# Joining attention bursts on TensorE and weaving strips of several products into them, with every engine's order written anew

## The chip, the cores and the metric

The kernel runs on one core of a Trainium2 chip. The metric is the time of one execution in microseconds (us), the median of several runs. A profile of one execution tells which engine did what and when.

## The reference

Four layers work on x, 2048 tokens of 448 numbers: sliding attention, a gated product, attention, a gated product. Each is added to its input after a layer norm without weights.

```python
def _A_ref(x, wqkv, wo):                 # H = 16 heads of Dh = 28; W, dil = 8, 2
    q, k, v = ...                        # x @ wqkv, split by head
    idx = pos[:, None] - (jnp.arange(W) * dil)[None, :]
    kg, vg = k[..., idx_c, :], v[..., idx_c, :]        # 8 keys and values for each token
    logits = jnp.einsum("bhsd,bhswd->bhsw", q, kg) * Dh ** -0.5     # masked where idx < 0
    o = jnp.einsum("bhsw,bhswd->bhsd", softmax(logits), vg)
    return o.transpose(...).reshape(B, S, D) @ wo
def _B_ref(x, w_gate, w_up, w_down):     # F = 1792
    return ((x @ w_gate) * (x @ w_up)) @ w_down
x = x + _A_ref(_layernorm(x), A_wqkv, A_wo)
x = x + _B_ref(_layernorm(x), B_w_gate, B_w_up, B_w_down)
# and both once more, with the same weights
```

Data are bf16.

## The kernel before

Tokens of even and odd position are kept apart, so that a key two positions back is the neighbour, and attention looks at a window of eight neighbours. Attention works on query blocks of 120 tokens (the first has 128), two blocks to a group, nine groups (0 to 8) in each of the two attention layers (0 and 2). The weight products work on chunks of 256 or 512 tokens. `SEQ` gives the chunks' order, in which the layers overlap: attention of chunk 1 stands ahead of the gated product of chunk 0, and so on.

**What each engine does.** TensorE computes the products for queries and keys (`WQK`), values (`WV`), attention's output (`wo_g`), gate and up (`WGU`) and down (`WD`). In all of these it is used as two tiles of 64 rows by 128 columns, and two matmuls, a pair, run at once (mode `R64`; line 351, function `pair`). For a group of attention it computes scores (line 826, `ps<-Qz,qk`, in `attn_front`) and then, of their exponentials, the attention values, AV for short (line 860, `ps<-E_sb,v_sb`, in `attn_back`). AV matmuls are 64 rows by 32 columns, eight tiles side by side; a group has 64 of them (group 0 has 32). Scores are in one of two forms, set by `WIDE_S`: a group named there has 32 matmuls in 64x64 tiles (group 0: 16), any other has 64 in 64x32 tiles (group 0: 32), each over fewer columns. Between scores and AV stand two exponentials on ScalarE (line 835) and two masks by VectorE (line 842). After the AV, copies (line 871), a sum (line 875), a shuffle of the denominators (line 885), a logarithm and an exponential (lines 886 and 887) and a product (line 898) give `oT`, which the output product reads. VectorE also does the layer norms (lines 571 to 592) and the sums into x (line 915); a gate result is copied out by ScalarE (line 951) and multiplied with the up result by VectorE (line 954). Copies of queries, keys (line 701) and values (line 793) out of PSUM go to ScalarE or VectorE, as the order says.

**Transposes.** A normed block of x is transposed for the products, in the head of the kernel by TensorE (line 606) and later by a DMA that SyncE issues (line 595). The last four heads' values reach their blocks through DRAM (lines 712 to 721), again by a transposing DMA.

**Bursts and strips.** A run of small attention matmuls between two products is a burst. Ahead of it and behind it TensorE changes tile size. In some bursts, strips of a product are woven in: a pair of the product is cut into eight 64x32 matmuls (line 354, `strip` in `pair`), which have the tile size of the attention matmuls, so the small ones and the strips follow each other without a change of size. The product that lends them is called the host; `alt` holds the strips of its first six pairs at most (`MAXALT`), and what is not in strips follows in pairs.

**What sets the order.** The order of every engine's operations is written out in the table `ORDER`, by operation numbers, and the PSUM banks of each TensorE operation in the table `BANKS`; `Sched.schedule` only reads them, and `emit` adds the waits that the dependences ask for. A word such as `545*1.2.4.5/434` in TensorE's order means: operation 545 (an AV) with host 434; after its first 8, 16, 32 and 40 matmuls comes one row of eight strips of 434 each. In this form a burst has one attention operation, or several before the cut (`762+776*...`), and one host.

Of the kernel before, what the change touches and what calls it, by code (L numbers as in the profile page):

```python
# [29 lines left out]
WIDE_S = ((0, 0), (0, 1), (0, 2), (0, 3), (0, 4), (0, 5))  # L30
MAXALT = 6
S_ORDER = (0, 4, 2, 6, 1, 5, 3, 7)
# [63 lines left out]
def grp_nc(g):  # L96
# [21 lines left out]
    ),  # L118
    "act": (
# [12 lines left out]
    ),  # L132
# [67 lines left out]
class Sched:  # L200
# [22 lines left out]
    def schedule(self):  # L223
# [9 lines left out]
        for e in self.ENGS:  # L233
            self.order[e] = []
            for w in ORDER[e].split():
# [4 lines left out]
                if k:  # L240
                    short, cut, host = seq, [8 * int(c) for c in k.split(".")], self.ops[int(host)]
                    got.append(host)
                    k = len(cut)
# [853 lines left out]
```

## Time and profile before

| | |
|---|---|
| three runs | 382.94, 383.2 and 385.03 us; median 383.2 |
| profiled execution, span from its first to its last instruction | 380.8 us |
| median less the span | 2.4 us |
| TensorE matmuls | 375.8 us busy (99%), 6322 |
| VectorE | 287.0 us busy (75%), 644 instructions |
| ScalarE | 203.6 us busy (53%), 389 instructions |
| granted TensorE clock, mean | 1.000 |

The profile has no time of its own execution besides the span, so the span stands beside the median of the runs.

Times are from the span's start. In a row of the timeline stand start, time, engine, line, instruction, output and inputs, the tile (rows*columns) and what streams through it, and how many instructions are merged in the row. The time of such a row ends with the last result of its last matmul, some 0.2 to 0.4 us after the next row may have begun, since matmuls are pipelined; so prices are taken from start to start. In the stretches' rows stand the stretch, its length, and for PE (matmuls), PEld (weight loads), DVE (VectorE), ACT (ScalarE) and POOL (GpSimd) the busy us with the count of instructions.

### The profile page before, as it was taken

What the parts mean: (1) busy time and instruction counts of PE and PEld (TensorE: products, weight loads), DVE (VectorE), ACT (ScalarE), POOL (GpSimd) and SP (SyncE); (2) the same over time, 40 slices, a digit from 0 to 9 for tenths busy, and PEclk for the clock granted to TensorE, in tenths of its full rate; (3) what the DMA queues carried; (4) which work ended last, traced back from release to release, by engine and by line L of the source; (5) the groups of instructions that cost most, each with busy time, mean ns of one, the idle gap of its engine ahead of it and who ended that gap; (6) DMA issues with size and microseconds to landing.
All of it is one profiled execution on the core that took longest, in us unless ns stands there. A gap on an engine that the chain in (4) does not pass through costs nothing.

```text
span 380.8 us, 14251 instructions
## 1 busy us (share of the span) xinstructions
PE 375.8 (99%) x6322; PEld 210.2 (55%) x6322; DVE 287.0 (75%) x644; ACT 203.6 (53%) x389; POOL 5.1 (1%) x25
## 2 busy tenths in 40 slices
PE   8999999999999999999999999999999999999997
PEld 4645587545445445444756765545555444446664
DVE  8988999999976786787677985637998598455323
ACT  5997987746426652564465525547744635133320
POOL 5000000000000000000000000000000000000000
DMA  8656533600611034031101125320125004140002
GB/s 263 163 148 177 106 94 95 80 19 3 99 29 33 2 65 58 16 67 26 32 14 34 20 43 101 39 45 4 28 34 74 3 2 78 23 120 26 3 2 98
DMA packets 54881, 22.50 MB, mean 59 GB/s; under 512 B 45012, under 2 KB 54820, under 8 KB 54820
## 3 DMA queue, kind: packets, MB, share of 16 engines
q1 hardware_dynamic: 54676, 21.53, 27.6%
q8 instruction: 50, 0.82, 0.9%
q14 instruction: 11, 0.09, 0.1%
q10 hardware_dynamic: 144, 0.06, 0.1%
HBM read 8.54 MB, written 2.71 MB: 30 GB/s over the span
## 4 chain that ended last, share of the span: by engine, by line
PE 94%; DVE 2%; ACT 1%; issue 1%; DMA 1%; SPq 0%; DVEq 0%
PE ps L351 85%; PE ps L354 3%; PE ps L860 2%; PE ps L826 2%; PE ps L966 1%; ACT E_sb L835 1%; DMA x_sb<-in_A_x_dram 1%; DVE xn_sb L592 1%; DVE st L571 0%; PE ps L606 0%; DVE Qz L812 0%; DVE R_sb L885 0%; DVE E_sb L842 0%; SPq L443 0%; DVE qk L701 0%
## 5 line engine op out<-in xcount | busy, mean ns | idle before, releaser
L351 PE MATMUL ps<-xnTb,WGU 64*128 64x512 bf16 (+1 forms) x1894 | 172.4, 332 | 0.0
L351 PEld LDWEIGHTS ps<-xnTb,WGU 64*128 64x128 bf16 x1894 | 92.0, 94 | 69.8 <-issue 1.4
L951 ACT ACTIVATE g_sb<-ps 128x512 bf16<-128x512 f32 (+1 forms) x140 | 70.1, 510 | 85.0 <-PE ps L351 65.5
L954 DVE TENSOR_TENSOR hT<-g_sb,ps 128x512 bf16<-128x512 bf16 (+1 forms) x140 | 78.2, 575 | 46.9 <-ACT g_sb L951 44.4
L351 PE MATMUL ps<-WD,hT 64*128 64x448 bf16 x812 | 82.8, 350 | 0.0
L351 PEld LDWEIGHTS ps<-WD,hT 64*128 64x128 bf16 x812 | 38.9, 94 | 34.7 <-DVE hT L954 0.3
L351 PE MATMUL ps<-xnTa,WQK 64*128 64x512 bf16 (+1 forms) x494 | 53.0, 353 | 0.5 <-DVE WQK L518 0.3
L915 DVE TENSOR_TENSOR x_sb<-x_sb,ps 128x448 bf16<-128x448 bf16 x62 | 37.2, 614 | 14.7 <-PE ps L351 14.4
L835 ACT ACTIVATE E_sb<-ps,shift_sb 128x1024 bf16<-128x1024 f32 (+1 forms) x36 | 37.0, 1068 | 12.6 <-PE ps L826 12.4
L571 DVE BATCH_NORM_STATS2 st<-x_sb 128x6 f32<-128x448 bf16 x64 | 38.6, 616 | 1.3 <-DMA x_sb<-in_A_x_dram 0.8
L592 DVE TENSOR_SCALAR xn_sb<-x_sb,mv,rstd 128x512 bf16<-128x512 bf16 (+1 forms) x64 | 35.2, 566 | 5.5 <-ACT rstd L576 5.5
L701 ACT ACTIVATE qk<-ps 128x1024 bf16<-128x1024 f32 (+1 forms) x29 | 27.1, 947 | 15.6 <-PE ps L351 15.6
L351 PEld LDWEIGHTS ps<-xnTa,WQK 64*128 64x128 bf16 x494 | 23.0, 94 | 21.6 <-DVE WQK L518 0.5
L351 PE MATMUL ps<-wo_g,oT 64*128 64x448 bf16 x250 | 28.6, 350 | 0.0
L842 DVE TENSOR_TENSOR E_sb<-E_sb,MK 128x1024 bf16<-128x1024 bf16 (+1 forms) x36 | 23.4, 658 | 5.3 <-ACT E_sb L835 5.2
L886 ACT ACTIVATE R_sb<-R_sb 128x480 f32<-128x480 f32 (+1 forms) x34 | 20.2, 601 | 9.6 <-DVE R_sb L885 9.6
L898 DVE TENSOR_TENSOR oT<-O_sb,R_sb 128x480 bf16<-128x480 f32 (+3 forms) x36 | 22.1, 624 | 4.3 <-ACT R_sb L887 4.2
L351 PE MATMUL ps<-WV,xnTa 64*128 64x336 bf16 (+3 forms) x252 | 24.2, 305 | 0.1
L885 DVE STREAM_SHUFFLE R_sb<-O_sb 128x480 f32<-128x480 f32 (+1 forms) x34 | 23.1, 692 | 0.0
L574 ACT ACTIVATE lnv<-mv,eps_sb 128x2 f32<-128x2 f32 (+1 forms) x33 | 9.3, 291 | 22.2 <-DVE mv L573 22.2
L887 ACT ACTIVATE R_sb<-R_sb 128x480 f32<-128x480 f32 (+1 forms) x34 | 20.2, 601 | 0.5
L871 ACT ACTIVATE O_sb<-ps 128x512 f32<-128x512 f32 (+3 forms) x18 | 9.8, 557 | 14.9 <-PE ps L860 14.9
(60 smaller groups left out, 214.8 us busy)
## 6 DMA issues: line engine op xcount, KB each, us to landing
out_dram<-x_sb SPq DMA_DIRECT2D x15, 112.0 KB, 1.8
x_sb<-in_A_x_dram SPq DMA_DIRECT2D x3, 448.0 KB, 5.8
hT<-in_A_wqkv_dram SPq DMA_DIRECT2D x4, 224.0 KB, 4.4
WGU<-in_B_w_gate_dram SPq DMA_DIRECT2D x4, 224.0 KB, 3.9
WGU<-in_B_w_up_dram SPq DMA_DIRECT2D x4, 224.0 KB, 3.8
WD<-in_B_w_down_dram SPq DMA_DIRECT2D x2, 448.0 KB, 4.2
WGU<-in_B_w_gate_dram SPq DMA_DIRECT2D x2, 336.0 KB, 4.8
WGU<-in_B_w_up_dram SPq DMA_DIRECT2D x2, 336.0 KB, 4.4
```

The source lines that it names most:

```text
L351: return lambda E: E.matmul(out(), lhs(), rhs(), start=start, stop=stop)
L571: sc.add("dve", one(lambda E, B=B: E.bn_stats(st6[:, B, :], x_sb[:, B, :]), ("bn", li, B)), 525.0, deps=[("x", li - 1, B)] + ([("xn", li - ...
L592: sc.add("dve", one(lambda E, B=B, dst=dst, src=src: E.tensor_scalar(dst, src, mv[:, B, 0:1], rstd[:, B:B + 1], ALU.subtract, ALU.mult), ( ...
L701: return E.activation(dst, src, ACT.Copy) if hasattr(E, "activation") else E.tensor_copy(dst, src)
L835: return E.activation(E_sb[:, slot, 2 * hp:2 * hp + 2, 0:w], ps[:, b0:b0 + 2, 0:w], ACT.Exp, bias=shift_sb[:, 0:1], scale=SCALE)
L842: return E.tensor_tensor(e, e, MK[:, kind, 0:nc].unsqueeze(1).unsqueeze(1).to_broadcast([128, 2, w // nc, nc]), ALU.min)
L885: sc.add("dve", one(lambda E: E.stream_shuffle(R_sb[:, rs, 0:w], O_sb[:, os_, 0:w], [DH] * 32), ("Rs", li, qb)), dve_est(w) + 20.0, deps=[ ...
L886: sc.add("act", one(lambda E: E.activation(R_sb[:, rs, 0:w], R_sb[:, rs, 0:w], ACT.Ln), ("Rl", li, qb)), act_est(w, False), deps=[("Rs", l ...
L898: return E.tensor_tensor(oT[:, :, a % HALF:a % HALF + z - a], O[:, :, a - tok:z - tok], R_sb[:, rs, 0:w].rearrange("p (h n) -> p h n", h=4 ...
L915: sc.add("dve", one(lambda E: E.tensor_tensor(x_sb[:, B, :], x_sb[:, B, :], ps[:, bk[w], 0:D], ALU.add), ("x", li, B)), dve_est(D), deps=[ ...
L951: sc.add("act", one(lambda E, gs=gs, bk=bk: E.activation(g_sb[:, gs, 0:nt], ps[:, bk[0], 0:nt], ACT.Copy), ("G", li, j, fc)), act_est(nt), ...
L954: sc.add("dve", one(lambda E, gs=gs, bk=bk, fc=fc: E.tensor_tensor(hT[:, fc, hs, 0:nt], g_sb[:, gs, 0:nt], ps[:, bk[1], 0:nt], ALU.mult), ...
```

## The change

Four things are changed.

1. `WIDE_S` holds group 0 of layer 0 alone. Groups 1 to 5 of layer 0 compute their scores with 64 matmuls in 64x32 tiles instead of 32 in 64x64 tiles.
2. `Sched.schedule` reads a wider form of a burst: several attention operations may be joined (`618+596`) and cut anywhere, and the strips may come from several hosts, each with the number of its pairs that are cut (`/729:2+484:6`).
3. The orders of all engines, SyncE's among them, are new, and with them the choice of ScalarE or VectorE for some copies and sums out of PSUM.
4. The banks are new.

The operations themselves, their sizes and their number are the same, but for the scores of point 1 and the pairs that are cut. In the built program TensorE has 6854 matmuls instead of 6322, 936 of them strips instead of 440. There are 31 bursts instead of 33, and the number of bursts without strips (the half groups included) falls from 15 to 6. The small product forms that are cut are now those of queries and keys, values, attention output, gate/up with 256 and 512 columns, and down.

```diff
-WIDE_S = ((0, 0), (0, 1), (0, 2), (0, 3), (0, 4), (0, 5))
+WIDE_S = ((0, 0),)
...
 ORDER = {
     "pe": (
...
-        "... 518 327 389 398 512 321 513 324 507 333 508 336 337 540*3.5/338 339 523 580 410 581 411 440 ... 545*1.2.4.5/434 ..."
-        "... 591*1.3.5/458 473 585 ... 596*1.2.4.5/654 669 681 666 482 613*2.4.5/483 660 ... 618*3.5/732 ..."
+        "... 518*4/281:1 327 333 388 512 389 398*1.3.4.6/507:2+513:2 508 336 337 580 540*1.2.3.4.5.6.7/338:1+339:6 410 581 523*2.4.6/411:3 ..."
+        "... 545*1.2.3.4.5.6.7/437:5+536:2 ... 591*1.3.4.6/477:3+558:1 ... 613*1.2.3.4.5.6.7/660:6+483:1 666 730 728 731 618+596*1.3.5.7.8.10.12.14/729:2+484:6 ..."
...
     "act": (
...
     "dve": (
...
     "sp": (
-        "... 511 90 427 429 510 433 516 431 576 577 578 515 583 579 574 ..."
+        "... 510 511 516 515 88 577 579 575 573 574 90 578 576 584 583 429 433 427 431 589 588 647 ..."
...
 BANKS = (
...
@@ schedule
                 w, _, tail = w.partition("*")
-                k, _, host = tail.partition("/")
+                k, _, tail = tail.partition("/")
                 got = [self.ops[int(i)] for i in w.split("+")]
                 seq = [(o, n) for o in got for n in range(len(o.ins))]
                 if k:
-                    short, cut, host = seq, [8 * int(c) for c in k.split(".")], self.ops[int(host)]
-                    got.append(host)
-                    k = len(cut)
-                    cut += [len(short)]
+                    short, cut = seq, [8 * int(c) for c in k.split(".")] + [len(seq)]
+                    hosts = [(self.ops[int(i)], int(n)) for i, n in (h.split(":") for h in tail.split("+"))]
+                    strips = [(o, i) for o, n in hosts for i in range(n)]
+                    assert len(strips) == len(cut) - 1
+                    got += [o for o, _ in hosts]
                     seq, a = [], 0
                     for i, z in enumerate(cut):
                         seq += short[a:z]
                         a = z
-                        if i < k:
-                            seq += [(host, host.alt[i][q]) for q in (S_ORDER if short[z - 1][0].acquire.n == 4 else range(8))]
-                    seq += [(host, n) for n in range(2 * k, len(host.ins))]
+                        if i < len(strips):
+                            o, j = strips[i]
+                            seq += [(o, o.alt[j][q]) for q in (S_ORDER if short[z - 1][0].acquire.n == 4 else range(8))]
+                    seq += [(o, n) for o, m in hosts for n in range(2 * m, len(o.ins))]
```

More of the change, by code (lines that the diff above doesn't have):

```diff
@@ L104 @@
     "pe": (
[13 rows of a table removed]
[15 rows of a table added]
     ),
     "act": (
[12 rows of a table removed]
[12 rows of a table added]
     ),
     "dve": (
[18 rows of a table removed]
[18 rows of a table added]
     ),
     "pool": (
-        "18 19 38 20 21 22 23 24 25 26 27 28 29 30 31 32 33 34 35 36 37"
+        "18 22 19 21 20 23 24 38 25 26 27 28 29 30 31 32 33 34 35 36 37"
     ),
     "sp": (
[5 rows of a table removed]
[5 rows of a table added]
     ),
```

128 rows, old and new, of tables (BANKS, ORDER) are left out of this document.

## The prediction

> **What bounds the kernel now.** I read the page first: busy shares, slices, chain of waits. Then the busy time by stretches, then the timeline of TensorE around single bursts, since the change is made of bursts.
>
> ```profile
> span 380.8 us, 14251 instructions
> ...
> PE 375.8 (99%) x6322; PEld 210.2 (55%) x6322; DVE 287.0 (75%) x644; ACT 203.6 (53%) x389; POOL 5.1 (1%) x25
> ...
> DVE  8988999999976786787677985637998598455323
> ...
> PE 94%; DVE 2%; ACT 1%; issue 1%; DMA 1%; SPq 0%; DVEq 0%
> ```
>
> TensorE is busy 99% of the span and 94% of the chain that ended last is TensorE's. So a microsecond less in TensorE's own stream is a microsecond less of span, as long as its inputs come in time. The row of 40 slices says where that may fail: VectorE is full for the first ten slices (95 us) and has room after that. By stretches (columns: stretch and length, then busy us and count of PE, PEld, DVE, ACT, POOL):
>
> ```profile
> 10.00:40.00 30.00, 29.53 (x544) 16.05 (x542) 27.08 (x80) 26.76 (x49) 0.00 (x0) 1.00 0.63 156
> 40.00:80.00 40.00, 39.30 (x882) 26.50 (x880) 39.18 (x92) 31.95 (x60) 0.00 (x0) 1.00 0.45 86
> 80.00:100.00 20.00, 20.00 (x354) 9.50 (x352) 18.27 (x40) 11.78 (x24) 0.00 (x0) 1.00 0.15 30
> ```
>
> From 40 to 80 us VectorE is busy 39.18 of 40. TensorE stands still for 0.47 us from 10 to 40 and 0.70 us from 40 to 80, then no more. So there are two bounds: both engines up to about 95 us, TensorE alone behind it.
>
> **What a burst costs.** A product runs in 64x128 tiles, two matmuls at a time (a pair). A burst is a run of small attention matmuls in 64x32 or 64x64 tiles. These rows (start, time, instruction) price bursts without strips:
>
> ```profile
> 37.41 0.64 PE L826 MATMUL ps<-Qz,qk 64*64 64x128 bf16 x32
> 37.98 0.82 PE L351 MATMUL ps<-xnTa,WQK 64*128 64x512 bf16 x6
> ...
> 199.75 0.68 PE L860 MATMUL ps<-E_sb,v_sb 64*32 64x64 bf16 x64
> 200.34 0.74 PE L826 MATMUL ps<-Qz,qk 64*32 64x64 bf16 x64
> 201.01 2.82 PE L351 MATMUL ps<-WD,hT 64*128 64x448 bf16 x28
> 203.67 0.93 PE L351 MATMUL ps<-xnTb,WGU 64*128 64x256 bf16 x14
> ...
> 284.69 1.50 PE L351 MATMUL ps<-WD,hT 64*128 64x448 bf16 x14
> 286.12 0.68 PE L860 MATMUL ps<-E_sb,v_sb 64*32 64x64 bf16 x64
> 286.74 0.60 PE L351 MATMUL ps<-WV,xnTa 64*128 64x336 bf16 x6
> ```
>
> A pair of 448 columns takes (203.67 - 201.01) / 14 = 0.19. The seven pairs at 284.69 should take 1.33, but the burst starts 1.43 later: entering a burst costs 0.10. From the first small matmul to the next product: 0.62 for 64 attention-value (AV) matmuls (286.12 to 286.74), 0.57 for 32 scores in 64x64 tiles (37.41 to 37.98), 0.67 for 64 scores in 64x32 tiles (200.34 to 201.01), 1.26 for AV and scores joined (199.75 to 201.01). With the entry: **0.72, 0.67, 0.77, 1.36**. So a lone group of scores gets 0.10 dearer in narrow tiles, and joining two bursts saves about 0.13.
>
> With strips, in the rows below, eight 64x32 matmuls of a product (L354) replace one of its pairs, between the small ones:
>
> ```profile
> 299.18 0.22 PE L826 MATMUL ps<-Qz,qk 64*32 64x64 bf16 x8
> 299.21 0.40 PE L354 MATMUL ps<-xnTb,WGU 64*32 64x512 bf16 x8
> 299.43 0.26 PE L826 MATMUL ps<-Qz,qk 64*32 64x64 bf16 x16
> 299.49 0.41 PE L354 MATMUL ps<-xnTb,WGU 64*32 64x512 bf16 x8
> ...
> 299.98 0.32 PE L826 MATMUL ps<-Qz,qk 64*32 64x64 bf16 x24
> 300.23 1.04 PE L351 MATMUL ps<-xnTb,WGU 64*128 64x512 bf16 x8
> 301.10 0.35 PE L351 MATMUL ps<-wo_g,oT 64*128 64x448 bf16 x2
> ...
> 311.80 0.22 PE L860 MATMUL ps<-E_sb,v_sb 64*32 64x64 bf16 x8
> ...
> 312.06 0.21 PE L860 MATMUL ps<-E_sb,v_sb 64*32 64x64 bf16 x8
> 312.09 0.40 PE L354 MATMUL ps<-xnTb,WGU 64*32 64x512 bf16 x8
> ...
> 312.82 0.27 PE L860 MATMUL ps<-E_sb,v_sb 64*32 64x64 bf16 x24
> 313.03 0.39 PE L351 MATMUL ps<-xnTb,WGU 64*128 64x512 bf16 x2
> ```
>
> Eight strips hold the array 0.22 (299.21 to 299.43), as long as the pair they replace ((301.10 - 300.23) / 4 = 0.22). So strips are free work, and the burst's price is what is left: 300.23 - 299.18 - 3 x 0.217 = 0.40 for scores, 313.03 - 311.80 - 4 x 0.217 = 0.36 for AV; with the entry **0.50 and 0.46**. Inside, eight small ones cost 0.03 (312.06 to 312.09), sixteen 0.06 (299.43 to 299.49), and the 24 at the end 0.21 to 0.25, of which 0.09 is theirs and 0.12 to 0.16 the way back to the wide tiles. So a burst cut finely costs 0.10 + 0.03 for each eight + about 0.13: **0.47 for 64, 0.59 for 96, 0.71 for 128**. More strips than three or four in a burst bring next to nothing; the gain lies in bursts that had none, and in joining.
>
> **The sum for TensorE.** I counted the bursts in both built orders; the product work is the same in both, strips included. Before, 33 bursts: the sixteen first scores (0.85) and a half AV (0.39), both unchanged in kind; 4 lone wide groups 4 x 0.67 = 2.68; one wide group joined to AV 1.17; 6 lone AV 4.32; 7 AV with strips 3.22; 10 scores with strips 5.0 (two of these have only one or two rows of strips: +0.2); an AV of 96 with 32 before its first strip 0.77; one half score 0.36; AV and scores joined 1.36. Sum 20.3. After, 31 bursts: 0.85 and 0.39; two lone scores, now narrow, 1.54; two joined pairs without strips 2.72; 10 scores at 0.48 and one with a single row of strips 0.57, 5.37; 10 AV with strips 4.60; one of 128 (two AV joined) 0.71, one of 96 0.59, AV and scores joined with strips 0.71, the half score with one row 0.35. Sum 17.8. **TensorE's stream is 2.5 us shorter**: about 1.2 of it in the first 95 us, 1.3 behind.
>
> Unknown in it: 96 strips are of 256 columns, which no row shows. Eight stream about 0.11 (half of 0.22), and the 16 matmuls of such a round must be issued in 0.11 + 0.03 = 0.14; the lone AV burst issues 64 in 0.62 - 0.13 = 0.49, so 16 in 0.12. It just fits: 0 taken; if the 64 scores' pace rules (0.67 - 0.13 = 0.54, 16 in 0.135) still 0; the far end is a round that hides nothing, 0.12 x 12 = 1.4, which I don't believe, as wider strips hide all of it. Below nothing it can't go.
>
> [...]
>
> **What the inputs allow.** VectorE and ScalarE run the same operations; some copies change engine (VectorE's total grows by about 1.5 us, almost all where it has room). I walked both built orders with the durations of this trace and asked how much of VectorE's queue must be done when TensorE has a given amount of product behind it. In the first 95 us the new order asks for 0.7 to 1.0 us less of VectorE at the same point of TensorE's work. So of the early 1.2, 0.9 gets through even if VectorE has no more gaps to give; the rest stays behind it. The way from scores to AV (two exponentials on ScalarE, a mask on VectorE) gets longer in TensorE's order in the tight early groups: the groups at 37 and 43 us have 4.2 and 3.7 us of TensorE work between them and their AV, and get 5.1 and 7.1.
>
> The transposes by DMA go the other way:
>
> ```profile
> L595 SPq DMA_TRANSPOSE xnTb<-xn_sb x32: 1221/1270/2398, 41.8 to 335.6; - x32
> ...
> DMA to landing us min/median/max: 2.4/3.0/4.8
> ```
>
> They feed a gate/up product (L351 `xnTb,WGU`). By the same walk, the last one of the second such chunk (75 us) has 3.0 us of lead over its first use instead of 5.1, the first chunk's (49 us) 3.3 instead of 5.4, the third's 3.9 instead of 8.0; some 0.8 comes on top as TensorE runs later than its bare sum. In SyncE's queue the v transposes that stood between them are moved ahead, so they issue 1.27 apart. Against a landing of 3.0 it holds; against 4.8 it doesn't. Behind each waiting transpose stand the next ones on SyncE, and behind the waiting product all of TensorE. I take 0, with 0 to 1.5 us at each.
>
> **Forecast.** 1.3 + 0.9 = 2.2 us less. The profiled execution's span of 380.8 lies 2.4 under the median of 383.2, which I leave as it is: **381.0 us**, by itself 380.2 to 381.8. About 0.5% (1.9 us: under 381.3 or over 385.1) is what a measurement of this kernel can tell from no change.
>
> **Rivals.** *VectorE keeps the early gain* (39.18 of 40 for it; its idle 2.9 us from 10 to 40 against): only the late 1.3 is left, 381.9, no change. *The early waits go too*: all of 2.5, and TensorE's idle 0.47 + 0.70 as the scores' way gets longer, 3.7 less, 379.5. For it, that the waits that I see are of that kind; against, that orders with less lead tend to make their own. *Late transposes, slower*: the three chunks at about 49, 75 and 100 us each wait on their last transpose. At landings of 4.8 against leads of 3.8, 4.1 and 4.7 it is 1.8 in all; with a transpose queued behind another, landing 1.3 later still, it is 1.0 + 1.3, 0.7 + 1.3 and 0.1 + 1.3, 5.7 in all, and VectorE, full there, can't catch up: 381.0 + 5.7 = 386.7. It turns the sign from 4.1 us on. For it the leads; against it the median of 3.0. *Issue bounds the rounds*: 256-column strips hide nothing, +1.4, 382.4, no change. [...] *That the change doesn't do what it says* is out: the built order has the five groups narrow and the strips where the list puts them.
>
> **Chances.** Forecast 0.44, VectorE 0.22, waits go 0.18, late transposes 0.13, issue 0.03. Faster by over 0.5%: all of the waits, two thirds of the forecast, a little of VectorE: 0.51. Slower: most of the transposes, 0.11, and 0.01 for the tails. The rest, 0.38, is no change. The range leaves out the best part of the waits going and the worse part of the transposes: 378.6 to 385.0.
>
> **What would show it.** TensorE's busy 99% again; bursts of 0.46 to 0.48 over their strips behind 95 us (first small matmul to next product, less 0.22, 0.19 or 0.11 for each eight strips, plus 0.10); the two early lone scores at 0.77; VectorE at 98% from 40 to 80 us; the first gate/up matmul of a chunk starting without a gap. I am wrong if idle time of TensorE before L351 `xnTb,WGU` shows at 49, 75 or 100 us, if rounds with 256-column strips take over 0.14, or if VectorE's idle share from 40 to 80 us grows while TensorE waits.

## The result: slower by 3.2 per cent, and the profile after

The changed kernel takes 395.75 us (median of six runs, 394.43 to 397.14) against 383.43 us for the kernel before (six runs): a ratio of 1.0322, 95% interval 1.0293 to 1.0351. Forecast were 381.0 us and a range of 378.6 to 385.0. The profiled execution is the longest of the six, 397.14 us; the granted clock of the six was 0.987 to 0.996.

The page of the profiled execution. All line numbers are four higher than before (L351 is L355, L354 is L358, L826 is L830, L860 is L864, L595 is L599).

```profile
span 395.3 us, 15371 instructions
...
PE 380.5 (96%) x6854; PEld 214.6 (54%) x6854; DVE 287.9 (73%) x646; ACT 205.6 (52%) x387; POOL 5.0 (1%) x25
...
PEclk9999899989999999999999999999999999999999
...
q8 instruction: 54, 0.88, 0.9%
...
PE 83%; DVE 6%; DMA 5%; ACT 3%; issue 2%; SPq 0%; ACTq 0%
```

TensorE fell from 99% to 96% of the span, and from 94% to 83% of the chain that ended last. In its place stand VectorE, DMA and "issue", time in which an engine waited for nothing that the profile shows. Two slices have a lower granted clock. The three stretches that the prediction quoted:

```profile
10.00:40.00 30.00, 29.68 (x636) 16.56 (x638) 26.26 (x74) 26.78 (x51) 0.00 (x0) 1.00 0.64 153
40.00:80.00 40.00, 35.91 (x1038) 24.38 (x1041) 34.28 (x83) 27.99 (x51) 0.00 (x0) 0.96 0.42 83
80.00:100.00 20.00, 16.54 (x264) 7.16 (x255) 14.45 (x33) 9.00 (x20) 0.00 (x0) 0.91 0.31 40
```

From 40 to 100 us TensorE stands still for 7.55 us (0.70 before), and VectorE, busy 39.18 of 40 before, does 34.28. So neither of the two bounds was lifted there: both engines wait.

The chain of waits, in order of time, gives the places (start, time, what):

```profile
44.76 1.88 issue
46.64 0.76 PE ps L355 x4
47.44 1.96 PE ps L355 x12
...
55.95 1.90 issue
...
79.26 4.70 DMA xnTb<-xn_sb
84.01 11.65 PE ps L355 x68
...
136.38 1.12 issue
...
256.52 3.98 DMA xnTa<-xn_sb
260.64 2.33 PE ps L355 x20
...
296.27 4.33 DMA xnTb<-xn_sb
300.65 3.58 PE ps L355 x36
```

I set the start of each matmul against TensorE's stream summed up at the prediction's prices, so the following shares are my sum and no row of the profile. In the kernel before, TensorE is 5.5 us behind that sum at the end, in the changed one 22.8. The 17.3 us between them arise at 40 to 60 us (6.4, before 1.3), 80 to 90 (5.3, before 0), 130 to 140 (1.6, before 0), 240 to 260 (2.1, before 0) and 290 to 340 (1.4, before 0), the rest in small pieces. Three kinds of place make it up: gaps without a wait (44.8, 56.0 and 136.4), late DMA transposes (84.0, 260.6 and 300.7), and a halved clock behind two of these gaps. The last by stretches, its column the one behind POOL's:

```profile
84.00:87.40 3.40, 3.39 (x18) 1.17 (x20) 0.04 (x1) 0.19 (x1) 0.00 (x0) 0.50 0.04 10
87.40:90.80 3.40, 3.40 (x34) 1.51 (x32) 2.06 (x5) 2.81 (x6) 0.00 (x0) 1.00 0.00 0
```

In these rows TensorE does 18 matmuls in the 3.4 us behind the wait at a granted clock of 0.50, and 34 in the next 3.4 us: 1.7 us lost. Behind the first gap (46.6 to 50.1 us) the clock is 0.54 and some 1.6 us are lost.

**The gaps without a wait.** Each of the three ends at the same place in TensorE's program: at an instruction whose index is 193 or 194 more than a multiple of 256 (a matmul is two instructions, the weight load and the matmul, and the waits between them count too: 2 x 6,854 and 157 others in the trace). The queue named "instruction" moves one packet of 16 KB for each 256 instructions: 54 in the page's row for the 13,865 instructions of TensorE in the trace, and before the change 50 for 12,782 (its page's row):

```profile
q8 instruction: 50, 0.82, 0.9%
```

So I read the gaps as missing instructions: the small matmuls are so short that a packet's 256 instructions are used up before the next packet is there. From the start of its first matmul to that of its last, the three packets ahead of the gaps took 1.45, 2.80 and 2.11 us. In the kernel before the shortest takes 2.85 us, and none has a gap behind it. Shortness alone doesn't decide: a packet of 2.69 us that ends at 170.8 us in the changed kernel left no gap; the transfer of the one behind it had begun 1.2 us before its own first instruction ran.

**The late transposes.** The four normalised blocks of the second chunk of layer 1 are issued for transposing by SyncE from 73.27 us on, and TensorE waits for the last:

```profile
73.27 7.29 SPq L599 DMA_TRANSPOSE xnTb<-xn_sb  x4
...
84.01 8.30 PE L355 MATMUL ps<-xnTb,WGU 64*128 64x512 bf16 x60 [3.46 <-DMA xnTb<-xn_sb]
```

VectorE ends the four at 72.8, 74.0, 75.3 and 76.6 us, but the issues start at 73.3, 75.5, 76.8 and 79.3, since each holds SyncE's queue for 1.3 to 2.4 us, and TensorE goes on 4.7 us after the last issue. TensorE arrives at 80.4, 3.8 us behind the last normalisation. 7.4 were needed. In the kernel before, the four issues were spread from 63.4 to 71.0 us, and TensorE came 5.9 us behind the last normalisation, without a wait:

```profile
68.42 1.30 SPq L595 DMA_TRANSPOSE xnTb<-xn_sb  x1
69.77 1.23 SPq L721 DMA_TRANSPOSE v_sb<-vt  x1
71.04 1.30 SPq L595 DMA_TRANSPOSE xnTb<-xn_sb  x1
...
75.40 3.83 PE L351 MATMUL ps<-xnTb,WGU 64*128 64x512 bf16 x34
```

This is not one unlucky chunk: in the kernel before no chunk's product comes less than 5.3 us behind its last normalisation; in the changed one six begin within 4.3 to 5.1 us of it, and three of these six (260.6, 300.7 and 334.1 us) show a wait.

**The bursts** cost about what was foretold:

```profile
37.88 0.68 PE L830 MATMUL ps<-Qz,qk 64*32 64x64 bf16 x64
38.50 1.50 PE L355 MATMUL ps<-xnTa,WQK 64*128 64x512 bf16 x12
...
295.60 0.68 PE L864 MATMUL ps<-E_sb,v_sb 64*32 64x64 bf16 x64
296.10 0.85 PE L830 MATMUL ps<-Qz,qk 64*32 64x64 bf16 x64
296.88 1.50 PE L355 MATMUL ps<-WD,hT 64*128 64x448 bf16 x14
...
304.16 0.22 PE L864 MATMUL ps<-E_sb,v_sb 64*32 64x64 bf16 x8
304.19 0.40 PE L358 MATMUL ps<-xnTb,WGU 64*32 64x512 bf16 x8
...
305.97 0.61 PE L355 MATMUL ps<-xnTb,WGU 64*128 64x512 bf16 x4
```

With 0.10 for the entry: 0.72 for a lone narrow score burst (0.77 foretold), 1.38 for AV and scores joined (1.36), and 305.97 - 304.16 - 5 x 0.217 - 2 x 0.19 (five strips of 512 columns, two of 448) + 0.10 = 0.45 for an AV with seven strips (0.46 to 0.48).

### The profile page after: what moved, and what is told of

The parts are those of the page before. It is cut to its first block, busy times and chain, and to the rows that moved or that the text cites. A ratio compares the mean times of both kernels' runs of the same rounds, so it can differ in the third digit from the quotient of the medians.

```text
span 395.3 us, 15371 instructions
## 1 busy us (share of the span) xinstructions
PE 380.5 (96%) x6854; PEld 214.6 (54%) x6854; DVE 287.9 (73%) x646; ACT 205.6 (52%) x387; POOL 5.0 (1%) x25
## 4 chain that ended last, share of the span: by engine, by line
PE 83%; DVE 6%; DMA 5%; ACT 3%; issue 2%; SPq 0%; ACTq 0%
PE ps L355 71%; PE ps L358 5%; DMA xnTb<-xn_sb 4%; PE ps L506 2%; PE ps L864 1%; ACT qk L705 1%; PE ps L970 1%; PE ps L830 1%; DVE x_sb L919 1%; DVE xn_sb L596 1%; DVE st L575 1%; DMA xnTa<-xn_sb 1%; DVE E_sb L846 1%; PE ps L610 0%; DVE Qz L816 0%
## 5 line engine op out<-in xcount | busy, mean ns | idle before, releaser
L355 PE MATMUL ps<-xnTb,WGU 64*128 64x512 bf16 (+1 forms) x1870 | 175.0, 335 | 4.6 <-DMA xnTb<-xn_sb 4.1
L355 PEld LDWEIGHTS ps<-xnTb,WGU 64*128 64x128 bf16 x1870 | 92.3, 94 | 76.4 <-DMA xnTb<-xn_sb 5.3
L955 ACT ACTIVATE g_sb<-ps 128x512 bf16<-128x512 f32 (+1 forms) x140 | 71.0, 511 | 114.0 <-PE ps L355 110.7
L958 DVE TENSOR_TENSOR hT<-g_sb,ps 128x512 bf16<-128x512 bf16 (+1 forms) x140 | 79.8, 575 | 48.6 <-ACT g_sb L955 46.0
L355 PE MATMUL ps<-WD,hT 64*128 64x448 bf16 x748 | 79.0, 349 | 0.0
L355 PE MATMUL ps<-xnTa,WQK 64*128 64x512 bf16 (+1 forms) x486 | 53.4, 355 | 1.2 <-DMA xnTa<-xn_sb 1.0
L355 PEld LDWEIGHTS ps<-WD,hT 64*128 64x128 bf16 x748 | 37.5, 94 | 30.0 <-issue 0.6
L839 ACT ACTIVATE E_sb<-ps,shift_sb 128x1024 bf16<-128x1024 f32 (+1 forms) x36 | 37.0, 1070 | 17.4 <-PE ps L830 17.3
L919 DVE TENSOR_TENSOR x_sb<-x_sb,ps 128x448 bf16<-128x448 bf16 x62 | 35.4, 616 | 12.8 <-PE ps L355 12.7
L355 PEld LDWEIGHTS ps<-xnTa,WQK 64*128 64x128 bf16 x486 | 22.9, 95 | 22.1 <-ACT g_sb L955 1.6
L705 ACT ACTIVATE qk<-ps 128x1024 bf16<-128x1024 f32 (+1 forms) x29 | 26.2, 920 | 9.7 <-PE ps L355 9.3
L355 PE MATMUL ps<-wo_g,oT 64*128 64x448 bf16 x230 | 27.1, 350 | 0.0
L355 PE MATMUL ps<-WV,xnTa 64*128 64x336 bf16 (+3 forms) x244 | 24.1, 313 | 2.1 <-issue 1.9
L875 DVE COPY O_sb<-ps 128x448 f32<-128x448 f32 (+3 forms) x18 | 11.2, 629 | 13.1 <-PE ps L864 13.1
L864 PE MATMUL ps<-E_sb,v_sb 64*32 64x64 bf16 (+1 forms) x1088 | 19.8, 192 | 0.0
```

What stands on the lines that cost most here:

```text
L355: return lambda E: E.matmul(out(), lhs(), rhs(), start=start, stop=stop)
L705: return E.activation(dst, src, ACT.Copy) if hasattr(E, "activation") else E.tensor_copy(dst, src)
L839: return E.activation(E_sb[:, slot, 2 * hp:2 * hp + 2, 0:w], ps[:, b0:b0 + 2, 0:w], ACT.Exp, bias=shift_sb[:, 0:1], scale=SCALE)
L864: ins.append((lambda E, b=b, c=c, o=o, vw=vw, eb=eb, eo=eo: E.matmul(ps[32 * b:32 * b + 32, bk[c], o:o + nc], vw, E_sb[64 * c:64 * c + 64, ...
L919: sc.add("dve", one(lambda E: E.tensor_tensor(x_sb[:, B, :], x_sb[:, B, :], ps[:, bk[w], 0:D], ALU.add), ("x", li, B)), dve_est(D), deps=[ ...
L955: sc.add("act", one(lambda E, gs=gs, bk=bk: E.activation(g_sb[:, gs, 0:nt], ps[:, bk[0], 0:nt], ACT.Copy), ("G", li, j, fc)), act_est(nt), ...
```

## The experiments

Two causes are to be told apart. **Starvation**: missing instructions make the gaps, and the wait at 84 us is their consequence, as VectorE, which is full there, loses what TensorE loses. **Order**: the wait at 84 us and those behind it are the new order's own, and the missing instructions come on top. The kernel before, run beside each set of experiments, took 383.05, 383.42, 383.13 and 383.26 us (medians); all ratios are to these.

### Moving the packets' borders

A number of tiny matmuls on zeros (64x32 tiles, 16 columns) goes ahead of the warm-up. It shifts the border of every packet and changes nothing else in TensorE's program, except that in the second and third run three warm-up matmuls are cut to 64 columns.

```diff
+PAD = 18     # first run; 102 in the second, 90 and 20 in the third and fourth
+pad = [((lambda E, c=c: E.matmul(ps[c:c + 32, 0, 0:16], warm[0:64, c:c + 32], warm[0:64, 0:16], ..., tile_position=(0, c))), None)
+       for c in [32 * (i % 4) for i in range(PAD)]] if n == 0 else []
-sc.add("pe", one(lambda E, n=n: E.matmul(...
+sc.add("pe", pad + one(lambda E, n=n: E.matmul(...
```

**The changed kernel, borders 36 instructions on.**

> The changed kernel with 18 tiny matmuls (36 instructions with their weight loads) ahead of its first warm-up matmul, so that all later instructions of TensorE stand 36 places further in their blocks of 256. Theory code fetch (TensorE's instructions come in blocks of 256, and a block that is used up in under about 3 us leaves it without instructions for 1 to 2 us): walked through the order, only one block is left under 2.7 us (2.2 us, at about 44 us), so the three waits of 1.3 to 2.2 us at 46, 57 and 137 us go, with the slow clock behind the first: 395.7 less 5.4 less 1.8, 388.5 or less; if the late transpose at 84 us was only their consequence, 382 to 384. Theory order (the new order itself keeps VectorE and the transposes too late): the shift changes nothing, 394 to 397.

Measured: 396.7 us (393.93 to 399.8), ratio to before 1.0357 (1.0281 to 1.0433).

```profile
47.05 0.26 PE L834 MATMUL ps<-Qz,qk 64*32 64x64 bf16 x16 [2.33 <-issue]
...
82.79 1.04 PE L357 MATMUL ps<-xnTb,WGU 64*128 64x512 bf16 x8 [3.79 <-DMA xnTb<-xn_sb]
```

The gaps at 57.9 and 137.5 us are gone, and the first has moved to the new border, in the middle of a burst. Another of 0.8 us has come at 205.1. So it is the border that decides, not the operation. By the median no time is won, where 388.5 or less was expected; but the four runs fall into two pairs, of 394 and of 399.5 us, and the profiled one, 393.93, is 3.2 us shorter than the changed kernel's profiled one. The wait for the transposes is as long as ever, 3.79. That speaks for the order.

**The changed kernel, borders 204 on.**

> The changed kernel with 102 tiny matmuls ahead (a shift of 204 instructions), three warm-up matmuls cut from 512 to 64 columns in return. Theory code fetch: four to six blocks run in 1.0 to 2.9 us at other places than before (about 53, 126, 160 and 285 us), each with a wait of 1 to 2.2 us, and no wait at 137: 393 to 399. Theory order: 394 to 397 with the waits at 46, 57 and 137 us where they were. The place of the waits tells, not the time.

Measured: 400.47 us, ratio 1.0455 (1.0424 to 1.0486).

```profile
29.72 0.19 PE L614 MATMUL ps<-ident,xn_sb 64*128 64x64 bf16 x1 [2.22 <-issue]
...
138.73 0.37 PE L360 MATMUL ps<-WD,hT 64*32 64x448 bf16 x4 [1.53 <-issue]
```

Gaps now stand at seven other borders (29.7, 51.9, 59.6, 138.7, 172.9, 207.9 and 302.1 us), and none at 46.6 or 57.9. That gaps stand at borders came true; which borders did not: of the four places named only the first has one, and one stands at 138.7, where none was expected. About 2.2 us of the loss is in the head, where the later loads of x land up to 2.5 us later, and isn't the borders'; why they do, no run shows.

**The kernel before, borders 180 on.**

> The kernel before with 90 tiny matmuls ahead (a shift of 180) and three warm-up matmuls cut to 64 columns. Theory code fetch: the joined AV and scores at 200 us now fill one block, used up in 0.6 to 1.3 us; a wait of about 2 us appears there that the kernel before doesn't have: 385 to 388. Theory order: 383 to 384.

Measured: 387.26 us, ratio 1.0114 (1.0097 to 1.013).

```profile
64.38 0.24 PE L864 MATMUL ps<-E_sb,v_sb 64*32 64x64 bf16 x12 [0.74 <-issue]
...
204.60 0.20 PE L830 MATMUL ps<-Qz,qk 64*32 64x64 bf16 x2 [0.66 <-issue]
```

The old order can be starved too: gaps that it never had, at the new borders. Of the 3.9 us that its span grew, about 2.0 are the head's again, the rest these gaps. So the expected time was met partly by luck: the gap at 200 us is a third of what was named, and the head was not in the sum.

**The kernel before with narrow scores.** The part of the change that needs no new order, alone:

```diff
-WIDE_S = ((0, 0), (0, 1), (0, 2), (0, 3), (0, 4), (0, 5))
+WIDE_S = ((0, 0),)      # and PAD = 20
```

> The kernel before with its own order, and point 1 of the change alone: scores of groups 1 to 5 of layer 0 in 64x32 tiles; 20 tiny matmuls ahead so that no block of 256 runs under 2.4 us. By the prices of the prediction each of the five lone bursts gets 0.10 dearer: 384 (+0.5), whichever theory holds; up to 385.5 if VectorE's tight queue multiplies it or the one block of 2.4 us starves.

Measured: 385.16 us, ratio 1.0055 (1.004 to 1.007).

```profile
29.52 0.30 PE L864 MATMUL ps<-E_sb,v_sb 64*32 64x64 bf16 x27 [1.26 <-issue]
```

By the price of a burst, narrowing costs 0.5 us; it cost 2.1 in the median, and the trace has three gaps at borders (29.5, 46.5 and 50.5 us), 1.9 us longer than the steps that they replace. So this kernel lost more than its bursts show. That the narrow tiles alone do it is not shown, as the 20 small matmuls ahead move the borders too.

Over the profiles of all 15 kernels of this study 37 of 774 borders have over 0.4 us from one instruction to the next. All but one of these were crossed 1.22 to 1.57 us after the new packet had landed (the other stands where the clock is halved), and no border at all was crossed sooner than 1.22 us after it. Of the packets used up in under 3.5 us, 26 of 58 have such a gap behind them, of those that lasted over 4.5 us 4 of 616. That settles what the gaps are.

### Thinning, and the order of one chunk

**The changed kernel, thinned.** Fewer instructions in the dense places, the order of all operations kept.

```diff
-WIDE_S = ((0, 0),)
+WIDE_S = ((0, 0), (0, 2), (0, 3), (0, 4))      # and PAD = 6
-241*2.5/344:2 ... 246*2.5/493:2
+241 344 ... 246 493
```

> The changed kernel with its densest stretches thinned, and nothing else moved: the three attention score operations of 30 to 45 us that host no strips (263, 371, 393) are computed in 16 large matmuls each as before the change instead of 64 small ones, the two bursts at 18 and 23 us give up their four strips, and 6 tiny matmuls on zeros stand ahead of the warm-up, so that by the durations measured no block of 256 TensorE instructions runs in under 2.9 us. If TensorE starved for instructions at 46.6, 57.9 and 137.5 us (2.19, 2.17 and 1.33 us), all three gaps go, and with the first one the slow clock behind it (1.8 us): 7.5 us. Theory O (the wait of 3.64 us at 84 us is the order's own: the four xn behind the transposes of that chunk end 3.6 us ahead of TensorE, VectorE is held up by as much as TensorE is): the wait at 80 to 84 us stays at 3 us or more, time 388 (386.5 to 389.5). Theory S (that wait is only the starvation's consequence): it falls under 1 us and the slow clock behind it goes too, time 383 (381.5 to 384.5). If the gaps are no starvation: they stay or are met elsewhere, time 393 to 397.

Measured: 393.11 us (390.96 to 396.51), ratio 1.0249 (1.0184 to 1.0315).

```profile
68.12 1.13 PE L357 MATMUL ps<-WD,hT 64*128 64x448 bf16 x9 [1.20 <-DVE xn_sb L600]
...
80.89 1.47 PE L357 MATMUL ps<-xnTb,WGU 64*128 64x512 bf16 x12 [3.47 <-DMA xnTb<-xn_sb]
```

The gaps of 44 to 58 us are gone and nothing stands in their place there, but the wait for the transposes is 3.47 as ever: the order's own, not a consequence. The theory's time was missed all the same, by 5 us. A new wait of 1.2 us stands at 68.1, another of 1.4 for transposes at 217.5, and the packet border at 132.7 has a gap of 1.38, although the packet ahead of it lasted 3.45 us: the transfer of the next began only 2.55 us into it.

**The same, with the chunk's normalisations first.**

```diff
 VectorE
-417 415 521 391 390 422 420 423 401 421 428 406 432 402 426 409 430 405
+417 415 391 390 428 426 422 420 423 421 432 430 401 406 402 521 409 405
 SyncE
-584 583 429 433 427 431
+429 427 433 431 584 583
```

> The same thinned kernel, and VectorE and the sync queue serve the second layer's second chunk first: of its four normalisations (xn 428, 426, 432, 430) two go ahead of the additions 391 and 390 and two directly behind their means, ahead of two shuffles, two products oT and one mask product (521), and their transposes go ahead of two unneeded V transposes in the sync queue. The last of the four normalisations should end some 2.6 us earlier. Theory O: the wait ahead of product 440 falls from over 3 us to under 1, and the slow clock behind it (1.7 us) goes, some 4 to 5 us below the thinned kernel, time 383.5 (382 to 385). Theory S: that wait has gone already, the same time as the thinned kernel within 0.7 us. If the product waits for something behind the transposes that ends as late, nothing is gained.

Measured: 390.6 us (389.07 to 392.52), ratio 1.0178 (1.013 to 1.0226); 2.5 us less than the kernel above, on the same chip, though the two kernels' runs overlap.

```profile
69.81 0.54 PE L364 MATMUL ps<-WD,hT 64*128 64x448 bf16 x3 [2.84 <-issue]
...
80.45 0.81 PE L364 MATMUL ps<-xnTb,WGU 64*128 64x512 bf16 x6
```

The last normalisation ends at 70.6 us, and TensorE begins product 440 at 80.45 without a wait. That wait is gone; the one at 68 to 70 us grew from 1.2 to 2.84, with 3.4 us of halved clock behind it (70.70 to 74.11 us, 1.7 us lost). Set against the kernel above, operation 580 at 74.1 us begins 3.3 us later and product 440 begins 0.4 us earlier: some 3.8 us are won at the product, and most of that had been lost just ahead of it. So the place was foretold right and the time (383.5) was not.

**The order without the thinning.** The two moves above in the changed kernel itself, all its small matmuls kept, and one load of weights (88) early.

> The changed kernel with all its small matmuls and strips, and only the leads of the second layer's second chunk mended: the four normalisations and their transposes first, and the weights 88 ahead of the V transposes. The starvation at 46.6, 57.9 and 137.5 us stays. Theory O: the wait of 3.64 us at 84 us and the 1.7 us of slow clock behind it go, 390.5 (389 to 392). Theory S (that wait is the starvation's consequence and moves elsewhere when it is mended here): 394 to 396.

Measured: 391.33 us (390.87 to 392.79), ratio 1.0202 (1.0151 to 1.0254).

```profile
81.02 0.20 PE L871 MATMUL ps<-E_sb,v_sb 64*32 64x64 bf16 x2 [2.02 <-issue]
81.16 0.36 PE L362 MATMUL ps<-wo_g,oT 64*128 64x448 bf16 x2
81.36 2.97 PE L362 MATMUL ps<-xnTb,WGU 64*128 64x512 bf16 x26
```

4.4 us less than the changed kernel, and no run of one is as long as the shortest of the other. The product at 81.36 does not wait; the last of its transposes was issued at 73.0 us. But the time was met partly by luck. Which borders starve has changed with the times alone: the gaps at 57.9 and 137.5, expected to stay, are gone, one of 2.02 us stands right ahead of the product, and the clock is not halved behind the first gap either. So the 4.4 us are not the price of this one wait.

**The kernel before, with one normalisation late.** The cross test: make the lead short where nothing else is disturbed.

```diff
 VectorE
-539 430 521 522 405 409 543 341
+539 521 522 405 409 543 341 430
```

> The kernel before, with one thing moved: VectorE computes the last normalisation of the same chunk (xn 430) behind six instructions that follow it now (two mask products, two products oT, one mask product, one addition), 3.8 us of VectorE's work. In the kernel before that xn ends at 69.5 us, its transpose is issued at 71.0 and TensorE begins the product at 75.4 without a wait. Theory O: the xn ends at about 73.3, the transpose issues at once and lands 4.4 to 4.7 us later at 77.9, so a wait of 2.5 us appears ahead of the product, with up to 1.5 us of slow clock behind it: 386 to 387. Theory S (a late transpose alone costs little, the order's slack takes it up): within 0.8 us of the kernel before.

Measured: 384.51 us, ratio 1.0021 (1.0008 to 1.0034), 1.1 us more than before.

```profile
77.37 1.90 PE L360 MATMUL ps<-xnTb,WGU 64*128 64x512 bf16 x16 [1.05 <-DMA xnTb<-xn_sb]
```

The normalisation ended at 74.4 us and its transpose, alone in the queue, landed 2.95 us later, not the 4.4 to 4.7 that I had taken from the changed kernel. The wait of 1.05 us is about the 1.1 us by which the median grew; the time lies between the two lines of the expectation. So a short lead costs, and at once. Four transposes in a row are worse than one, first by the 2.7 us that the last waits for its issue in the changed kernel.

### Following the waits

The wait at 68 to 70 us is ahead of operation 336, the down product, for which TensorE waits until four quarters of its weights have landed. The change had moved two of them back in SyncE's queue: 88 is issued at 62.1 us instead of 55.3, 90 at 66.9 instead of 58.7.

**Weights 88 early** (`503 88 510 511 516 515 577` in place of `503 510 511 516 515 88 577`).

> As the thinned kernel with the normalisations first (390.6), and one line of the sync queue moved: the first down-projection weights (88) are issued ahead of the V transposes 510, 511, 516 and 515, some 7 us earlier. If the new wait of 3.1 us at 69.8 us, for which the profile names no releaser, is for these weights: it goes, and the slow clock of 1.9 us behind it with it, time 386.5 (385 to 388). If it is the instructions that come late there: it stays, 390 to 391.

Measured: 388.81 us, ratio 1.0121 (1.0062 to 1.018).

```profile
68.88 0.35 PE L364 MATMUL ps<-WD,hT 64*128 64x448 bf16 x1 [1.74 <-DVE mv L588]
```

The wait is still there: not this quarter. The traces name the other one: in the thinned kernel, in the one with the normalisations first and in this one, operation 336 begins 0.20 us after quarter 90 has landed (67.92 and 68.12 us, 69.61 and 69.81, 68.68 and 68.88).

**Weights 90 early too** (`503 88 90 510 ...`, ahead of the zero fills that wait for the projections).

> As the one before with the weights 88 early (388.8), and the third quarter of the down-projection weights (90) is issued early too, ahead of the V transposes and of the zero fills of the next window, which wait for the projections. TensorE waits for all four quarters at once ahead of 336, and 90 was issued 3.4 to 3.9 us before that wait ended in each of the three thinned kernels (64.7 to 68.1, 64.5 to 68.6, 66.1 to 69.8 us). If 90 is what the wait of 2.04 us at 68.9 us is for: it goes, time 386.8 (385.5 to 388). If it is the instructions that come late there: it stays, 388 to 389.5.

Measured: 390.32 us (389.1 to 390.85), ratio 1.0166 (1.0102 to 1.0231).

```profile
67.51 0.56 PE L364 MATMUL ps<-WD,hT 64*128 64x448 bf16 x4 [0.56 <-issue]
...
74.75 0.55 PE L364 MATMUL ps<-wo_g,oT 64*128 64x448 bf16 x4 [0.85 <-ACT E_sb L850]
```

The wait for the weights is gone: 0.56 us are left, at a packet's border. But 0.85 us of waiting for attention's way through ScalarE and VectorE stand behind it, and the time is not lower. The expectation of 386.8 was wrong in time, right in place. Operation 336 now begins at 66.61 us, 5.6 us after quarter 90 has landed.

**Two products let others pass** (on TensorE `1190 1274` for `1274 1190` and `1298 1241 1394` for `1394 1298 1241`).

> As the one with the normalisations first, and on TensorE two products that wait for late transposes let ready work pass: 1190 (a gate and up product) goes ahead of 1274 (the product that waits 1.14 us at 260.6) and 1298 and 1241 go ahead of 1394 (which waits 0.68 us at 300.7). Theory O: 1.5 us (1.0 to 2.0) below the one without these two moves, 382. If the two waits only move to the next product that needs the same chunk or the next free bank: no gain, within 0.5 us of it.

Measured: 392.45 us, ratio 1.022 (1.018 to 1.026), against 390.6 without, so neither line of the expectation. The first move leaves 0.15 us of a wait of 0.67; behind the second the AV at 301.4 us waits 1.41 for VectorE, where it didn't wait before.

**Several leads at once**, first with the weights 88 alone:

> The thinned kernel with the normalisations first, with these leads added: the sync queue issues the first down-projection weights (88) ahead of three V transposes, as early as before the change; 1190 goes ahead of 1274 on TensorE; VectorE serves 756 ahead of 880 (which waits for a transpose), the mean of 1377 ahead of 1216 and 1384 and 1386 ahead of 1228; ScalarE computes 1379 ahead of 1289; and the joined burst at 173 us keeps three of its six strips, with 12 tiny matmuls ahead of the warm-up, so that no block of 256 instructions runs in under 3.3 us by the durations measured. Theory O plus starvation (everything the change lost is late work of other queues and missing instructions, its bursts being as cheap as counted): the stream by the durations measured is 369.5 us against 371.3 of the kernel before, waits of 7 us against 5.5, so the time is 383 (381.5 to 385), the same as the kernel before within 0.4 per cent. If the bursts themselves cost more than counted, or a wait taken away comes back in another place each time: 387 or more.

Measured: 388.75 us (387.39 to 390.57), ratio 1.0134 (1.009 to 1.0179). Then with 90 too and without a move that had made a wait of its own:

> The last one with 1190 ahead of 1274 on TensorE, 756 ahead of 880 on VectorE, two reciprocal roots (719 and 1379) ahead of the V copies next to them on ScalarE, three strips fewer in the joined burst at 173 us and 12 tiny matmuls ahead of the warm-up (no block of 256 instructions under 3.3 us). Against the kernel that had all leads but 90 (388.75): the wait at 68.4 (1.36), the one at 288.6 (1.97, made by a move that is left out here) and half of the one at 126.0 (0.8) go, so 384.7 (383 to 386). A late packet of instructions at 131 us (1.6) may stay. If waits only change place: 388 or more.

Measured: 388.81 us (388.49 to 391.16), ratio 1.0134 (1.0086 to 1.0181).

```profile
124.98 0.61 PE L364 MATMUL ps<-xnTa,WQK 64*128 64x512 bf16 x4 [1.13 <-DMA xnTa<-xn_sb]
...
129.97 0.36 PE L367 MATMUL ps<-WD,hT 64*32 64x448 bf16 x1 [1.25 <-issue]
```

Both times the pessimistic line of the expectation came true, in its second form: waits taken away come back elsewhere, while the bursts cost what was counted. In this last kernel TensorE is 14.6 us behind its summed stream (22.8 in the changed kernel, 5.5 before), most of it in ten steps of 0.5 to 1.6 us: late transposes (125.0, 292.7 and 326.5), the way of attention (70.1, 74.4, 154.5), one late packet (130.0), and three others. Its stream is 1.9 us shorter than that of the kernel before, as counted, so the bursts' gain is there and the waits use it up almost five times over. No version that I ran beats the kernel before.

**What the runs settle.** By the medians the thinning alone gave 2.6 us (its runs of 390.96 to 396.51 overlap the changed kernel's, so this is not clear of the noise), the order of one chunk with the weights 88 gave 4.4, thinning and order 5.2, and all leads 7.0 of the 12.3. The other 5 us are located, in the gaps named above, but not taken away by a run: whether this order can be mended at all, or VectorE and the DMA queues bound it there, stays open. Also open is why some packets are asked for late: the transfer of the next packet began between 1.2 us ahead of the first instruction of the one then running and 2.5 us behind it (5th and 95th percentile), and I found no rule for that. In three traces (the order without the thinning, and the two with several leads) it began 4.4 to 4.6 us behind it and left a gap after a packet of some 5 us, so long packets are not safe either.

## Why the prediction was wrong, point by point

- **TensorE's stream, 2.5 us shorter: right as far as the bursts show.** The burst prices came out within 0.05, but for the joined pair at 43 us (42.98 to 44.44, 1.56 with the entry instead of 1.36), right ahead of the first gap. Four rounds of 256-column strips that stand by themselves take 0.138 to 0.158; two of them are over the 0.14 named as a sign, but by 0.02, some 0.2 us over 12 rounds, so that term (0, at most 1.4) was near enough.
- **532 more matmuls, with no term for their number: right for the array by the rows, and it hid the question.** In the quoted rows 64 small matmuls take 0.62 us, under 10 ns each, and the sum prices the bursts, not the number of instructions. What they cost is their supply: 256 instructions last 1.45 us in the changed kernel's densest packet, and none of the 774 borders was crossed sooner than 1.22 us behind the next packet's landing. No term of the sum held this, and no rival named it: it was put at nothing without a row. In the changed kernel it is 4.8 us of gaps (1.88, 1.90 and 0.98 idle in TensorE's rows) and 1.6 of slow clock.
- **"Against a landing of 3.0 it holds; against 4.8 it doesn't. I take 0": this step failed.** The lead was right: 3.0 + 0.8 foretold, 3.8 measured. The need was wrong. It counted the landing from the issue of one transpose, at its median, and took the issues to be 1.27 apart; they were 2.2, 1.3 and 2.4 apart. The last issue came 2.7 us behind its data, and TensorE went on 4.7 behind that. Needed were 7.4 us; cost 3.46 and 1.7 of halved clock. With the normalisations and transposes ahead in their queues the product began without a wait (80.45 and 81.36 us). The prediction named this chunk and put the price at 1.0 + 1.3 in the rival with 0.13, which had the sign and one of its three chunks right. It looked for short leads in the chunks up to 100 us only; the ones at 260.6 and 300.7 us cost another 1.5.
- **"Of the early 1.2, 0.9 gets through": wrong.** Nothing got through: the stretch from 40 to 100 us lost 6.85 us more of TensorE's time than before. VectorE had little to give, but it had more to lose: while TensorE stood still it ran dry, 34.28 of 40.
- **Weights: not looked at.** The two loads moved back behind the v transposes are hidden in the changed kernel by its own gaps (TensorE comes late), and are the next wait as soon as these are thinned.
- **The signs named for being wrong** were the right ones in part: idle time of TensorE ahead of `xnTb,WGU` showed at 84 us for the 75 us chunk, not for the first and third, and VectorE's idle share grew while TensorE waited. (Of the three chances for faster, slower and no change, 0.51, 0.12 and 0.38, the sum is 1.01.)

## What to carry to other kernels

When a change cuts an engine's work into many short instructions, price their supply as well as their run time: find how many instructions a packet holds and compare the shortest time in which one is used up, over all of the program, with the fetch; and look at when each fetch begins, since a late one starves a longer packet too (4.4 to 4.6 us into packets of some 5 us in three traces here). When an order is written anew, list for every transfer, over the whole length, what lies between its data being ready and its use, and hold it against the worst case with all neighbours of its queue ahead of it, not the median. A stream summed from busy time is a floor (TensorE was 5.5 us behind it before the change, 22.8 in the changed kernel): where two engines are full, mending one wait tends to uncover the next, as it did in most of the runs above.

## What the runs showed of the hardware

- TensorE's instructions came in packets of 16 KB, one for each 256 instructions, during the run: 54 in the changed kernel, from 12.9 to 385.7 us, and 50 in the kernel before. In the 15 traces a transfer took 0.88 to 1.8 us, median 1.08, and the first instruction of a packet never ran sooner than 1.22 us after it.
- Behind some gaps of TensorE the granted clock was 0.50 for 3.41 us, and not by the gap's length alone: behind 1.88 and 3.46 us in the changed kernel it was, behind 1.90 us (57.85) in the same kernel and 3.47 us in the thinned one it wasn't (granted clock 1.000 over the whole run of the latter). The two such stretches of the changed kernel begin at 46.43 and 83.98 us, 37.55 apart, which is 11 times 3.41. What decides which gap is followed by one, no run shows.
- A DMA transpose of a normed block, alone in SyncE's queue, landed 2.9 us after its issue (with one normalisation late) and 3.0 and 3.6 us after it (the kernel before, issues at 68.4 and 71.0 us). The last of four in a row took 4.7 us in the changed kernel and in the thinned one and 3.8 with the normalisations first, and each of the four held the queue for 1.3 to 2.4 us.
